# Attention units with transposed sums: which operand of the normalisation is read with a stride

## The chip, the cores and the metric

The kernel runs on one core of a Trainium2 chip. The metric is device time in microseconds (us) of one execution; what is quoted as the time before is the median of three runs. The engines are named as in the profile: PE is TensorE (matmuls), PEld its weight loads, DVE is VectorE, ACT is ScalarE, POOL is GpSimd, SP is SyncE, whose queue issues most DMAs.

## The reference

Everything is bf16, with S = 2048 tokens, D = 512 features, H = 32 heads of Dh = 128, and a key and value cache of 2048 positions for each head.

```python
xn = layernorm(x)                                   # [2048, 512]
q  = (xn @ wq) -> [32 heads, 2048, 128]
p  = softmax(q @ k_cache^T * Dh**-0.5)              # over 2048 keys
s  = (p @ v_cache) -> [2048, 4096] @ wo             # back to [2048, 512]
g  = silu(B(xn))     # B: a token-shifting mixer (w1, w2) and an MLP 512 -> 1792 -> 512 (w3, w4), both residual
out = x + s * g
```

## The kernel before, in words

The first part (until about 130 us) makes `xn`, its transpose `xnT` and most of the gate `g`. The rest is attention, and that is where the change lies.

Attention is cut into 128 units. `units` lists them by group `g` of four heads (8 groups), block `qt` of 512 queries (4 blocks) and head `hh` in the group, the head running fastest. A unit has eight slots. Slot n of the main loop belongs to unit u = n // 8 and has the place p = n % 8 in it. In each slot PE makes two score matmuls for unit u (`s_slot`: keys as weights, `qT` of 128x512 streamed through, into one PSUM tile `ps_s`), ACT takes the exponential of the 128x1024 scores into a tile `pT` (L291), and PE makes two matmuls of an earlier slot with the values as weights (`pv_slot`, into `ps_o`). In the middle part these run ten slots late (`lag = 2 * LAG`). PE's spare places go to the projection of a coming unit's queries (`q_mm`, four matmuls a unit) and to the output projection of finished units (`wo_slot`, `wo_mm`, four matmuls a unit). `pin` fixes the order of each engine: what is written first in the loop is first on its engine, and nothing overtakes.

DVE sums the exponentials: `add_first`, `add_next` and `add_last` (L297, L302, L307, L308) fold a unit's `pT` tiles into `acc[:, 0, :]`, 128 keys by 512 queries. What is still missing is the sum over the 128 partitions, its reciprocal, and that reciprocal spread over all partitions. There are two ways to it. Units outside `TURN` use four tiny matmuls (`sums`). The 96 units of `TURN` (12 to 107, so all of them in whole blocks of four heads) use a DMA transpose: `turn` (L333) transposes `acc` into `tT`, so that query j * 128 + p lies in partition p, place j; `turned_sums` (L338 to L342) sums each row on DVE into `sm`, a 128x4 tile, takes the reciprocal `rc`, and writes it to a DRAM tile `dr`; `bcast` (L346) reads `dr` back as one row of 512 numbers into every partition of `rb`. In that row, query j * 128 + p stands in column p * 4 + j.

`norm` (L358) then multiplies the unit's output `ps_o` (128x512, fp32, in PSUM, queries in their natural order) by `rb` (fp32, in SBUF) and writes bf16 into one quarter of `oT`, which holds the four heads of a block. As the columns of `rb` are ordered p * 4 + j in TURN units, it is read there with a step of four elements; `ps_o` and `oT` are walked in a row. For a TURN unit u the DVE work falls like this: `turn(u)` in slot 3 of unit u + 1, `turned_sums(u)` in slot 0 and `bcast(u)` in slot 1 of unit u + 2, and `norm(u)` in slot 7 of unit u + 2. On DVE, the order around it is: `add_next` of the running unit (slot 6), `norm` (slot 7), `wo_post` of an output tile (L411, slot 7), then at slot 0 of the next unit `turned_sums` of the next unit (L338, L340) and `add_last` (L302, L307, L308), and in slot 3 the copy of the next queries (`q_copy`, L275).

When the four heads of a block are done, `wo_mm` takes, for each 128 tokens `ts` of the block and each head, the columns `ts * P:(ts + 1) * P` of `oT` as matmul weights against `wo`. `ps_o` has two PSUM buffers, so the first `pv_slot` of a unit (slot 2 of unit u + 3 for the buffer of unit u) waits until `norm` of the unit two before has read its buffer. The keys are used as weights with a step as well: `s_slot` views `kT` as `"d (i p j) -> d i j p"` with j = 4, so its 128 weight columns lie four elements apart.

Loads of the next group's keys and values (`load_k`, a DMA transpose, and `load_v`) are issued on SP's queue at set slots around each change of group, between `dr`, `rb` and `tT`.

Of the kernel before, what the change touches and what calls it, by code (L numbers as in the profile page):

```python
# [17 lines left out]
def kernel(  # L18
# [16 lines left out]
    P = nc.NUM_PARTITIONS  # L35
# [9 lines left out]
    QT = Sq // 512  # L45
# [5 lines left out]
    HG = 4  # L51
    NG = H // HG
# [55 lines left out]
    def mm(out, lhsT, rhs, start, stop):  # L108
        pin(nc.tensor.matmul(out=out, lhsT=lhsT, rhs=rhs, start=start, stop=stop))  # L109
# [14 lines left out]
    TURN = range(3 * HG, NU - 5 * HG)  # L124
    PV0, PV1 = 2 * HG, NU - 5 * HG + 3
    NS = NU * SPU
    kTs, vBs, wqs, wos, oTs, st = {}, {}, {}, {}, {}, {}
# [221 lines left out]
    def norm(u):  # L349
        g, qt, hh = units[u]  # L350
        s = st.pop(u)
        if hh == 0:
            oTs[(g, qt)] = pB.tile([P, HG, 512], BF16, tag="oT", bufs=2, name="oT")
        o, rb, to = s["o"][:], s["rb"][:], oTs[(g, qt)][:, hh, :]
        if u in TURN:
            o, to = (x.rearrange("k (j p) -> k j p", j=4) for x in (o, to))
            rb = rb.rearrange("k (p j) -> k j p", j=4)
        pin(nc.vector.tensor_tensor(out=to, in0=o, in1=rb, op=ALU.mult))  # L358

    wo_box = {}  # L360
    sacc = {}

    def load_wo(h):
        wos[h] = pB.tile([P, D], BF16, tag="wo", bufs=2 * HG, name="wo_h")
        pin(nc.sync.dma_start(out=wos[h][:], in_=A_wo[h * Dh:(h + 1) * Dh, :]))

    def wo_mm(g, t, hhs):
        if hhs[0] == 0:
            wo_box[0] = psX.tile([P, D], FP32, tag="xm", name="ps_wo")
        oT = oTs[(g, t // 4)]  # L370
        ts = t % 4
        for hh in hhs:
            mm(wo_box[0][:], oT[:, hh, ts * P:(ts + 1) * P], wos[g * HG + hh][:], hh == 0, hh == HG - 1)

    fin = {}

# [73 lines left out]

    def last_wo(ts, ps, hhs=(0, 1, 2), stop=False):
        for hh in hhs:
            mm(ps, oTs[(NG - 1, QT - 1)][:, hh, ts * P:(ts + 1) * P], wos[(NG - 1) * HG + hh][:],
               hh == 0, stop and hh == HG - 2)

    def last_act(ps, scale):
# [200 lines left out]
    def norm_queue(u):  # L657
        norm(u)
        gg, qq, hh = units[u]
        if hh == HG - 1:  # L660
            wo_todo.extend((gg, 4 * qq + ts) for ts in range(4))
            if gg == NG - 1 and qq not in LATE:
                fin_load(4 * qq)
# [3 lines left out]
    def wo_slot(part, n, each=2):  # L667
        gg, t = wo_todo[0]
        if part < HG // each:
            wo_mm(gg, t, tuple(range(part * each, (part + 1) * each)))  # L670
            return
        wo_todo.popleft()
        wo_post(gg, t, n)
        if gg == NG - 1 and t % 4 < 3 and t + 1 not in fin and t // 4 not in LATE:
            fin_load(t + 1)

    q_plan = defaultdict(list)
    for v in range(1, NU):
        if v not in made:
            for dc in range(DC):  # L680
                k = dc - 1 if v - 2 in TURN else dc // 2
                q_plan[(v - 1) * SPU + k].append((v, (dc,)))

    for n in range(UB * SPU):
        u, p = divmod(n, SPU)
# [45 lines left out]
    for p in range(SPU):  # L731
        s_slot(UB, p)
        pv_run(n + p)
        if p == 0:
            add_last(UA)
        if p < 2:
            wo_slot(p, n + p)
        if p == 3:
            norm(UB - 2)
            sums(UA)  # L740
            wo_slot(2, n + p)
        if p == 4:
            bcast(UA)
            add_first(UB)
        if p == 6:
            add_next(UB, 2)
# [5 lines left out]
    def bank(pl, tag, **kw):  # L752
        return pl.tile([P, D], FP32, tag=tag, name="ps_w", **kw)[:]

    ps = {0: bank(psX, "xm")}
# [6 lines left out]
    late_sums(UB, [acc[:, i, :] for i in range(2)], True, False)  # L762
    late_sums(UB, [pT[:, i, :] for i in range(2, 4)], False, True)
    norm(UA)
    late_rc(UB)
    late_o(UB)
    last_wo(0, ps[0], stop=True)
    late_wo(UB, 0, wl[0])
    wl[1] = bank(psO, "ps_o")
    late_wo(UB, 1, wl[1])  # L770
    last_wo(1, ps[1])
    wl[2] = bank(psX, "xa")
    wl[3] = bank(psO, "ps_o")
# [9 lines left out]
    tb[1] = last_act(wl[1], rc[:, 1:2])  # L783
    tb[2] = last_act(wl[2], rc[:, 2:3])
    last_wo(2, ps[2])
    join(1)
    last_wo(3, ps[3])
# [49 lines left out]
```

## Time and profile before

| | |
|---|---|
| median of three runs | 1260.08 us (1258.32, 1260.08, 1260.21) |
| the profiled execution's own time | 1261.13 us |
| its span in the profile | 1259.4 us |
| PE busy | 1239.5 us, 98% |
| ACT busy | 1100.7 us, 87% |
| DVE busy | 1033.0 us, 82% |
| granted TensorE clock | 0.999 |

The span is what the profile covers from the first to the last instruction; the execution's own time is 1.7 us longer. A line such as `L358 DVE TENSOR_TENSOR oT<-ps_o,rb 128x512` names the source line, the engine, the operation, and the tiles written and read; behind `x` stands the count. A matmul row of some 379 ns is the latency of one matmul; the next one starts long before, so the pitch between starts, not this number, tells how fast PE goes. The stage in which TURN units are normalised goes from about 258 to 1091 us.

### The profile page before, as it was taken

What the parts mean: (1) busy time and instruction counts of PE and PEld (TensorE: products, weight loads), DVE (VectorE), ACT (ScalarE), POOL (GpSimd) and SP (SyncE); (2) the same over time, 40 slices, a digit from 0 to 9 for tenths busy, and PEclk for the clock granted to TensorE, in tenths of its full rate; (3) what the DMA queues carried; (4) which work ended last, traced back from release to release, by engine and by line L of the source; (5) the groups of instructions that cost most, each with busy time, mean ns of one, the idle gap of its engine ahead of it and who ended that gap; (6) DMA issues with size and microseconds to landing.
All of it is one profiled execution on the core that took longest, in us unless ns stands there. A gap on an engine that the chain in (4) does not pass through costs nothing.

```text
span 1259.4 us, 16202 instructions
## 1 busy us (share of the span) xinstructions
PE 1239.5 (98%) x5782; PEld 598.3 (48%) x5899; DVE 1033.0 (82%) x1430; ACT 1100.7 (87%) x1113; POOL 34.4 (3%) x91
## 2 busy tenths in 40 slices
PE   8999999999999999999999999999999999999997
PEld 4444444444444444444444444444444444444443
DVE  7621567788888988888898988988898999988888
ACT  4344889999998999999999999999999999898886
POOL 4320000000000000000000000000000000000000
PEclk9999999999999999999999999999999999999999
DMA  6492012444345423454354524553364434452222
GB/s 155 106 169 72 10 30 46 82 91 93 60 72 97 110 58 76 88 110 84 47 101 94 104 50 76 96 116 69 55 101 102 101 66 82 92 97 54 68 56 59
DMA packets 224945, 103.86 MB, mean 82 GB/s; under 512 B 176928, under 2 KB 208160, under 8 KB 224864
## 3 DMA queue, kind: packets, MB, share of 16 engines
q1 hardware_dynamic: 221648, 100.07, 40.9%
q0 software_dynamic: 672, 1.84, 0.8%
q8 instruction: 46, 0.75, 0.3%
q10 hardware_dynamic: 2544, 0.92, 0.3%
q14 instruction: 35, 0.29, 0.1%
HBM read 67.90 MB, written 2.36 MB: 56 GB/s over the span
## 4 chain that ended last, share of the span: by engine, by line
PE 88%; DMA 5%; DVE 5%; ACT 1%; issue 1%; DVEq 0%; ACTq 0%; SPq 0%
PE ps_s L109 36%; PE ps_o L109 33%; PE ps_q L109 8%; PE ps_wo L109 8%; DMA rb<-dr 3%; PE ps_m L109 2%; DMA dr<-rc 2%; DVE oT L358 1%; DVE acc L302 1%; DVE sacc L411 1%; DVE sm L338 1%; DMA tT<-acc 0%; PE ps_warm L109 0%; ACT pT L291 0%; ACT xnT L199 0%
## 5 line engine op out<-in xcount | busy, mean ns | idle before, releaser
L291 ACT ACTIVATE pT<-ps_s 128x1024 bf16<-128x1024 f32 x1024 | 1034.6, 1023 | 79.1 <-PE ps_s L109 31.4
L109 PE MATMUL ps_s<-qT,kT 128*128 128x512 bf16 x2041 | 607.5, 379 | 0.6
L109 PE MATMUL ps_o<-pT,vb 128*128 128x512 bf16 x1962 | 588.9, 379 | 2.3 <-DVE oT L358 1.8
L302 DVE TENSOR_TENSOR acc<-acc,pT 128x2048 bf16<-128x2048 bf16 x255 | 309.2, 1213 | 73.4 <-ACT pT L291 68.6
L109 PEld LDWEIGHTS <-kT 128*128 128x128 bf16 x2048 | 231.0, 113 | 226.2 <-issue 0.8
L109 PEld LDWEIGHTS <-vb 128*128 128x128 bf16 x2048 | 200.2, 98 | 228.3 <-issue 3.0
L109 PE MATMUL ps_wo<-wo_h,oT 128*128 128x512 bf16 x492 | 177.8, 379 | 2.1
L109 PE MATMUL ps_q<-xnT,wq_h 128*128 128x512 bf16 x481 | 172.7, 379 | 2.1
L297 DVE TENSOR_TENSOR acc<-pT 128x2048 bf16<-128x2048 bf16 x128 | 155.7, 1216 | 6.1 <-ACT pT L291 5.9
L358 DVE TENSOR_TENSOR oT<-ps_o,rb 128x512 bf16<-128x512 f32 x127 | 124.4, 980 | 30.5 <-DMA rb<-dr 29.7
L307 DVE TENSOR_TENSOR acc<-acc 128x1024 bf16<-128x1024 bf16 x127 | 87.9, 692 | 4.3
L275 DVE CAST qT<-ps_q 128x512 bf16<-128x512 f32 x112 | 76.5, 683 | 0.3 <-PE ps_q L109 0.3
L109 PEld LDWEIGHTS <-oT 128*128 128x128 bf16 x508 | 48.5, 98 | 56.6 <-DVE oT L358 1.1
L109 PEld LDWEIGHTS <-wq_h 128*128 128x128 bf16 x484 | 47.2, 98 | 56.2 <-issue 0.2
L411 DVE TENSOR_TENSOR sacc<-ps_wo,sacc 128x512 f32<-128x512 f32 x96 | 65.5, 683 | 3.2 <-PE ps_wo L109 2.7
L338 DVE TENSOR_REDUCE sm<-tT 128x4 f32<-128x512 bf16 x96 | 64.7, 674 | 1.8 <-DMA tT<-acc 1.8
L308 DVE TENSOR_TENSOR acc<-acc 128x512 bf16<-128x512 bf16 x127 | 54.0, 425 | 4.3
L242 ACT ACTIVATE h2T<-ps_s 128x1024 bf16<-128x1024 f32 x28 | 28.6, 1023 | 24.1 <-PE ps_s L109 24.1
L109 PE MATMUL ps_s<-xn2T,w_sb 128*128 128x512 bf16 x219 | 48.6, 379 | 0.3
L109 PEld LDWEIGHTS <-w_sb 128*128 128x128 bf16 x304 | 29.7, 98 | 34.6 <-issue 2.1
L109 PEld LDWEIGHTS <-h2T 128*128 128x128 bf16 x224 | 21.5, 98 | 25.0 <-issue 0.2
L109 PE MATMUL ps_m<-w_sb,h2T 128*128 128x512 bf16 x106 | 31.0, 379 | 0.5
(73 smaller groups left out, 333.5 us busy)
## 6 DMA issues: line engine op xcount, KB each, us to landing
rb<-dr SPq DMA_DIRECT2D x127, 256.0 KB, 4.2
vb<-in_A_v_cache_dram SPq DMA_DIRECT2D x64, 256.0 KB, 3.3
wo_h<-in_A_wo_dram SPq DMA_DIRECT2D x32, 128.0 KB, 3.6
wq_h<-in_A_wq_dram SPq DMA_DIRECT2D x28, 128.0 KB, 3.3
w_sb<-in_B_w_dram SPq DMA_DIRECT2D x9, 256.0 KB, 5.0
kT<-in_A_k_cache_dram SPq DMA_TRANSPOSE x128, 3.3
xl<-in_A_x_dram SPq DMA_DIRECT2D x16, 128.0 KB, 3.7
dr<-rc SPq DMA_DIRECT2D x127, 2.0 KB, 1.4
```

The costliest lines, as they stand in the source:

```text
L109: pin(nc.tensor.matmul(out=out, lhsT=lhsT, rhs=rhs, start=start, stop=stop))
L242: pin(nc.scalar.activation(out=h2[c, f][:], in_=ps[:], func=ACT.Gelu_apprx_tanh))
L275: pin(nc.vector.tensor_copy(out=qT[:], in_=st[u].pop("psq")[:]))
L291: pin(nc.scalar.activation(out=s["pT"][-1][:, jj:jj + 2, :], in_=sps[:], func=ACT.Exp, scale=SCALE))
L297: pin(nc.vector.tensor_tensor(out=s["acc"][:], in0=s["pT"][0][:], in1=s["pT"][1][:], op=ALU.add))
L302: pin(nc.vector.tensor_tensor(out=a[:], in0=a[:], in1=st[u]["pT"][i][:], op=ALU.add))
L307: pin(nc.vector.tensor_tensor(out=a[:, 0:2, :], in0=a[:, 0:2, :], in1=a[:, 2:4, :], op=ALU.add))
L308: pin(nc.vector.tensor_tensor(out=a[:, 0, :], in0=a[:, 0, :], in1=a[:, 1, :], op=ALU.add))
L338: pin(nc.vector.tensor_reduce(out=sm[:], in_=s["tT"][:], axis=mybir.AxisListType.X, op=ALU.add))
L358: pin(nc.vector.tensor_tensor(out=to, in0=o, in1=rb, op=ALU.mult))
L411: pin(nc.vector.tensor_tensor(out=sa, in0=ps[:], in1=sa, op=ALU.add))
```

## The change

In TURN units, `norm` walks all its operands in the order of `rb`: `rb` and the output quarter of `oT` in a row, and `ps_o` with a step of 128 fp32 elements (512 bytes) from one element to the next, four elements to a turn. So the columns of `oT` of a TURN unit stay in the order p * 4 + j. A new function `o_cols` gives `wo_mm` and `last_wo` the 128 columns of a token tile: of a TURN unit every fourth column, of other units the same contiguous slice as before. The number and order of instructions, and what each waits for, stay as they were. `last_wo` handles the last block, which is outside TURN.

```diff
@@ norm
         if u in TURN:
-            o, to = (x.rearrange("k (j p) -> k j p", j=4) for x in (o, to))
-            rb = rb.rearrange("k (p j) -> k j p", j=4)
+            o = o.rearrange("k (j p) -> k p j", j=4)
+            rb, to = (x.rearrange("k (p j) -> k p j", j=4) for x in (rb, to))
         pin(nc.vector.tensor_tensor(out=to, in0=o, in1=rb, op=ALU.mult))
@@
+    def o_cols(g, qt, hh, ts):
+        o = oTs[(g, qt)][:, hh, :]
+        if (g * QT + qt) * HG + hh in TURN:
+            return o.rearrange("k (p j) -> k j p", j=4)[:, ts, :]
+        return o[:, ts * P:(ts + 1) * P]
+
     def wo_mm(g, t, hhs):
...
-        oT = oTs[(g, t // 4)]
         ts = t % 4
         for hh in hhs:
-            mm(wo_box[0][:], oT[:, hh, ts * P:(ts + 1) * P], wos[g * HG + hh][:], hh == 0, hh == HG - 1)
+            mm(wo_box[0][:], o_cols(g, t // 4, hh, ts), wos[g * HG + hh][:], hh == 0, hh == HG - 1)
@@ last_wo
-            mm(ps, oTs[(NG - 1, QT - 1)][:, hh, ts * P:(ts + 1) * P], wos[(NG - 1) * HG + hh][:],
+            mm(ps, o_cols(NG - 1, QT - 1, hh, ts), wos[(NG - 1) * HG + hh][:],
```

## The prediction

> **What bounds the kernel now.** I read the page's busy times first, then the stage of the TURN units (a window from the first to the last `turned_sums`), PE's timeline in it, the waits, and last the chain of waits.
>
> ```profile
> span 1259.4 us, 16202 instructions
> ...
> PE 1239.5 (98%) x5782; PEld 598.3 (48%) x5899; DVE 1033.0 (82%) x1430; ACT 1100.7 (87%) x1113; POOL 34.4 (3%) x91
> ```
>
> ```profile
> 258.40:1083.50 825.10, 819.31 (x3738) 396.35 (x3813) 732.34 (x966) 779.72 (x763) 0.00 (x0) 1.00 0.45 86
> ```
>
> The second row's columns after the length are PE, PEld, DVE, ACT and POOL busy with counts, granted clock, DMA share, GB/s. PE is busy in 819.31 of 825.10 us at a granted clock of 1.00, DVE in 732.34. A busy PE need not be at its peak, so the pitch of its matmuls has to be read:
>
> ```profile
> 599.53 0.59 PE L109 MATMUL ps_s<-qT,kT 128*128 128x512 bf16 x2
> 599.96 0.59 PE L109 MATMUL ps_o<-pT,vb 128*128 128x512 bf16 x2
> 600.40 0.38 PE L109 MATMUL ps_q<-xnT,wq_h 128*128 128x512 bf16 x1
> 600.61 0.59 PE L109 MATMUL ps_s<-qT,kT 128*128 128x512 bf16 x2
> 601.04 0.59 PE L109 MATMUL ps_o<-pT,vb 128*128 128x512 bf16 x2
> 601.48 0.38 PE L109 MATMUL ps_wo<-wo_h,oT 128*128 128x512 bf16 x1
> 601.69 0.59 PE L109 MATMUL ps_s<-qT,kT 128*128 128x512 bf16 x2
> 602.12 0.38 PE L109 MATMUL ps_o<-pT,vb 128*128 128x512 bf16 x1
> ```
>
> From 599.53 to 602.12 start 2+2+1+2+2+1+2 = 12 matmuls: 216 ns each, the same for every kind of weight. A unit has 16 score, 16 value, 4 query and 4 output matmuls, so 40 x 0.216 = 8.63 us. DVE's turn in the same place:
>
> ```profile
> 602.30 1.22 DVE L297 TENSOR_TENSOR acc<-pT 128x2048 bf16<-128x2048 bf16 x1
> 604.46 1.22 DVE L302 TENSOR_TENSOR acc<-acc,pT 128x2048 bf16<-128x2048 bf16 x1 [0.93 <-ACT pT L291]
> 605.60 1.07 DVE L358 TENSOR_TENSOR oT<-ps_o,rb 128x512 bf16<-128x512 f32 x1
> 606.60 0.68 DVE L411 TENSOR_TENSOR sacc<-ps_wo,sacc 128x512 f32<-128x512 f32 x1
> 607.20 0.67 DVE L338 TENSOR_REDUCE sm<-tT 128x4 f32<-128x512 bf16 x1
> ...
> 610.93 1.22 DVE L297 TENSOR_TENSOR acc<-pT 128x2048 bf16<-128x2048 bf16 x1
> ```
>
> One unit takes 610.93 - 602.30 = 8.63 us here too, and DVE idles 0.93 us of it, waiting for ACT. So PE's stream sets the pace, without a gap, and DVE has 0.93 us a unit to spare. Time can be won only where PE itself waits. The waits from 258 to 1092 us name those places (us in total, times, longest):
>
> ```profile
> DVE oT L358 <- DMA rb<-dr: 25.6, 38, 2.6
> ...
> PE ps_o L109 <- DVE oT L358: 1.8, 2, 1.6
> ...
> PE ps_sum L109 <- DVE qT L275: 0.7, 1, 0.7
> ```
>
> The first row matters only through the second: `norm` waits 38 times for its broadcast, but PE waits for `norm` twice. The two larger stalls by PE's starts:
>
> ```profile
> 399.21 0.59 PE L109 MATMUL ps_s<-qT,kT 128*128 128x512 bf16 x2
> 401.40 0.59 PE L109 MATMUL ps_o<-pT,vb 128*128 128x512 bf16 x2 [1.60 <-DVE oT L358]
> ...
> 1086.67 0.59 PE L109 MATMUL ps_o<-pT,vb 128*128 128x512 bf16 x2
> 1087.92 0.27 PE L109 MATMUL ps_sum<-ones_t,acc 128*128 128x1 bf16 x4 [0.66 <-DVE qT L275]
> ```
>
> Two matmuls after 399.21 the next was due at 399.64 and came at 401.40: 1.76 us lost. Likewise it was due at 1087.10 and came at 1087.92: 0.82 lost. The other wait for `norm` is 1.8 - 1.6 = 0.2. All that DVE costs PE in this stage is 0.2 + 1.76 + 0.82 = 2.8 us.
>
> **The change, part by part.** (1) *The multiply of `norm`.* Its duration in units 0 to 11 (nothing strided) and in the 96 TURN units (`rb` read with a 16-byte step), from the answers for line L358 in the two stages (ns, min/median/max):
>
> ```profile
> L358 DVE TENSOR_TENSOR oT<-ps_o,rb x12: 678/682/684, 151.4 to 252.8; 128x512 bf16<-128x512 f32 x12
> ...
> L358 DVE TENSOR_TENSOR oT<-ps_o,rb x96: 1054/1073/1094, 267.8 to 1090.3; 128x512 bf16<-128x512 f32 x96
> ```
>
> The strided SBUF read costs 1073 - 682 = 391 ns, 0.76 ns for each of 512 elements. The change takes it away and puts a read of PSUM with a 512-byte step in its place. No row of this trace reads PSUM with a step. From below: 682 ns, the step free; less than that is excluded, since 682 is the price with all three operands in a row. From above, the nearest row is `rb`'s own step: 1073 again; were a longer hop twice as dear, 682 + 2 x 391 = 1464. I take 682: the read of PSUM is another memory's, and in the 12 unstrided rows it is not what the multiply waits for, since the add of L411 above, also 128x512 with one operand in PSUM, takes the same 0.68 us. That is the weakest step, and both ends go into the range. At 682, DVE loses 96 x 0.391 = 37.5 us of busy time, nearly all of it behind PE.
>
> [...]
>
> (2) *What is late next.* A shorter `norm` brings everything behind it on DVE forward: `wo_post` (L411), `turned_sums` (L338, L340), and so the issue of `dr` and `rb` on SP. The chain of waits shows that these close a ring ahead of the 1.76 us stall:
>
> ```profile
> 335.78 0.99 DVE oT L358
> 336.77 0.60 DVE sacc L411
> 337.37 0.60 DVE sm L338
> 338.20 1.39 DMA dr<-rc
> 339.61 5.82 DMA rb<-dr
> 345.45 1.08 DVE oT L358
> ...
> 395.00 5.27 DMA rb<-dr
> 400.29 1.07 DVE oT L358
> ```
>
> Each `norm` starts when `rb` lands, and its end releases the sum that the next `rb` needs. From 345.45 to 400.29 there are six turns of 9.14 us against PE's 8.63: the ring falls behind while key and value loads share the queues, until PE waits. With 0.39 us less a turn it takes 8.75; six turns end 2.3 us earlier and the last `norm` 0.39 earlier still, more than the 1.76 lost. This supposes that `rb` lands earlier when issued earlier. If the landing is held by the loads around it, only the last `norm` counts: 0.39. At 1087 us the wait is for the query copy (L275), which stands behind `norm` on a DVE without idle time: 0.39 of 0.82 certain, more if that `rb` too comes earlier. The wait of 0.2 goes.
>
> (3) *The weights of the output projection.* 24 blocks x 4 token tiles x 4 heads = 384 loads read every fourth column. The keys are read with the same step:
>
> ```profile
> L109 PEld LDWEIGHTS <-kT x2048: 110/113/120, 127.1 to 1245.1; 128*128 128x128 bf16 x187
> ...
> L109 PEld LDWEIGHTS <-oT x380: 97/98/98, 262.3 to 1079.3; 128*128 128x128 bf16 x190
> ```
>
> Such a load takes 113 in place of 98 ns, 15 more, and lies beside a matmul of 216: in PE's timeline above, matmuls on `kT` start at the same pitch as the rest. I take nothing; if that cover were gone, 384 x 0.015 = 5.8 us. No load can get shorter. (4) The bf16 write stays in a row, and no DMA, wait or order changes: nothing.
>
> Sum: lowest gain 0.2 + 0.39 + 0.39 = 1.0 us, highest 2.8; I take 0.2 + 1.76 + 0.39 = 2.35. Against the profiled execution's own 1261.13 us (1.7 of it outside the span) that is 1258.8. The shown runs have their median at 1260.08 and the fastest at 1258.32, as far under 1261.13 as these stalls are long (2.8), so I read the runs' differences as more or less of the same stalls. A median without most of them stands at about **1258.7**, 1.4 under the median now.
>
> **The rivals.** *The PSUM read costs what the SBUF read did*: `norm` stays near 1073 and nothing moves, 1260.1. For it speaks that the step is longer than `rb`'s; against it, that it is another memory. *The read is dearer than before, and the ring falls further behind*: at 1464 each turn of the ring takes 0.39 more, so the stall at 399 grows by 7 x 0.39 = 2.7 and the other two by 0.39 each: 3.5 more, 1260.08 + 3.5 = 1263.6, slower; it decides from any duration over 1073. [...] *DVE becomes the bound*: over 1.07 + 0.93 = 2.0 us of `norm`, DVE's turn passes 8.63 and all 96 units pay; at 682 + 4 x 391 = 2246 ns that is 96 x 0.24 = 23 us, 1283. Nothing in the trace shows a price that high. *The strided weights stall PE*: 1260.08 + 5.8 = 1265.9; the rows of `kT` speak against it, and for it only that an output load sits singly between other kinds.
>
> **How the numbers follow.** The forecast, a free PSUM step, gets 0.55; the same price 0.16; the dearer read 0.12; the DVE bound 0.06; the weights 0.11. The forecast alone ranges from 1261.13 - 2.8 = 1258.3 to 1261.13 - 1.0 = 1260.1. The range goes down to 1257.2, as a run may vary by about another 1 us below that, as the three shown do among themselves, and up to 1263.6, which leaves out the DVE bound and the weights (0.17). About 0.2%, 2.5 us, is what a measurement of this kernel can tell from no change. In the forecast a gain over that comes only if all stalls go and the runs before are like the profiled one (2.8 of 1261.13 is 0.22%): 0.20 of its 0.55, the rest is same. The second rival is same; of the dearer read 0.10 is slower, of the weights 0.09, the DVE bound wholly. Faster 0.20; slower 0.10 + 0.06 + 0.09 = 0.25; same 0.55.
>
> **What would show it.** Right: the TURN rows of L358 at about 682, DVE busy near 995 us, weights from `oT` at about 113 ns with PE's pitch still 216, the wait of PE for L358 gone, the idle time of L302 behind ACT longer. Wrong: L358 at 1073 or above, PE waiting for L358 more than twice, a pitch over 216 around `ps_wo`; or L358 at 682 and the stall near 399 us still there, which would say that `rb`'s landing, not its issue, closes the ring.

## The result and the profile after

The kernel after takes 1258.01 us (median of 21 runs, 1257.45 to 1259.76) where the kernel before, in the same comparison, takes 1260.06 (21 runs, 1258.32 to 1262.11): ratio 0.9985, 95% interval 0.9979 to 0.9991. That is 2.0 us less, clear of noise and within 0.2%. The profiled executions took 1261.13 before and 1258.32 after.

The page's head, after (span, then busy time, share and count of each engine):

```profile
span 1256.5 us, 16202 instructions
...
PE 1238.1 (99%) x5782; PEld 604.2 (48%) x5899; DVE 997.1 (79%) x1430; ACT 1100.6 (88%) x1113; POOL 34.4 (3%) x91
```

DVE is busy 36 us less (1033.0 to 997.1), and the span is 2.9 us shorter. The multiply, from the answer for its line from 258 to 1092 us, its last instance being one outside TURN (ns, min/median/max), and the loads from `oT` in the same window:

```profile
L358 DVE TENSOR_TENSOR oT<-ps_o,rb x97: 676/684/693, 268.4 to 1091.6; 128x512 bf16<-128x512 f32 x97
...
L109 PEld LDWEIGHTS <-oT x384: 97/113/116, 262.4 to 1086.0; 128*128 128x128 bf16 x192
```

So the PSUM read with a step of 512 bytes costs nothing: 684 ns against 682 with all operands in a row. The weight loads went from 98 to 113 ns. The waits of that window, after (us in total, times, longest):

```profile
DVE acc L302 <- ACT pT L291: 78.0, 89, 0.9
DVE acc L297 <- ACT pT L291: 23.6, 68, 0.8
DVE oT L358 <- DMA rb<-dr: 10.6, 13, 1.5
```

No row is left in which PE waits for DVE. The freed time stands in the first two rows, where DVE waits for ACT. `norm` waits for `rb` 13 times in place of 38. The chain of waits from 330 to 405 us, before and after, tells the rest; its head gives the share of each line:

```profile
by line: DMA rb<-dr 41.6%; DMA dr<-rc 20.6%; DVE oT L358 9.6%; DVE sacc L411 5.9%; DVE sm L338 5.6%; PE ps_s L109 4.0%; PE ps_o L109 3.7%; issue 2.4%; DVE rc L340 1.8%; DVE acc L302 1.6%; ACT pT L291 1.4%; PE ps_wo L109 1.2%; PE ps_q L109 0
```

```profile
by line: PE ps_s L109 40.3%; PE ps_o L109 38.0%; PE ps_wo L109 11.2%; PE ps_q L109 10.2%; issue 0.5%
```

Before, the chain there went through the ring of `norm`, sums and broadcast; after, it is PE's stream alone. DVE's timeline, after, at the two ends of the six units that took 9.14 us each before:

```profile
345.14 0.69 DVE L358 TENSOR_TENSOR oT<-ps_o,rb 128x512 bf16<-128x512 f32 x1 [0.60 <-DMA rb<-dr]
...
396.26 0.68 DVE L358 TENSOR_TENSOR oT<-ps_o,rb 128x512 bf16<-128x512 f32 x1
```

The first of these `norm`s waited 0.60 us for its broadcast. Six units on this is made up: 51.12 us against PE's 6 x 8.63 = 51.78. The pace of the ring itself can't be read from them, as `norm` hardly waits for `rb` any more. The answers for `rb` from 330 to 405 us, before and then after (DVE's waits in us and times; time from issue to landing):

```profile
  DMA rb<-dr: 8.4, 7
...
DMA to landing us min/median/max: 3.5/4.2/5.8
```

```profile
  DMA rb<-dr: 0.6, 1
...
DMA to landing us min/median/max: 3.3/3.5/5.8
```

The broadcasts themselves landed faster in the profile after. Not all of that is the work of the shorter `norm`: in e1_weights below, whose `norm` still takes 1073 ns, the median there is 3.6. The stalls at 399 and at 1087 us are gone (PE's timeline, after):

```profile
399.26 0.59 PE L109 MATMUL ps_o<-pT,vb 128*128 128x512 bf16 x2
...
1084.53 0.59 PE L109 MATMUL ps_o<-pT,vb 128*128 128x512 bf16 x2
1084.96 0.27 PE L109 MATMUL ps_sum<-ones_t,acc 128*128 128x1 bf16 x4
```

The first sums of a unit outside TURN start 0.43 us after the two matmuls ahead of them, at PE's pitch. The rows also tell where the 2.9 us were won. The matmul that came at 401.40 before comes at 399.26, 2.14 earlier, and the sums that came at 1087.92 come at 1084.96, 2.96 earlier: 2.1 us up to the first place, 0.8 from there to the second, and nothing behind it.

### The profile page after: what moved, and what is told of

Read it like the earlier page. It is cut to its first block, busy times and chain, and to the rows that moved or that the text cites. A ratio compares the mean times of both kernels' runs of the same rounds, so it can differ in the third digit from the quotient of the medians.

```text
span 1256.5 us, 16202 instructions
## 1 busy us (share of the span) xinstructions
PE 1238.1 (99%) x5782; PEld 604.2 (48%) x5899; DVE 997.1 (79%) x1430; ACT 1100.6 (88%) x1113; POOL 34.4 (3%) x91
## 4 chain that ended last, share of the span: by engine, by line
PE 95%; DVE 2%; DMA 1%; ACT 1%; issue 1%; POOL 0%; SPq 0%; DVEq 0%; ACTq 0%
PE ps_s L109 39%; PE ps_o L109 36%; PE ps_q L109 9%; PE ps_wo L109 9%; PE ps_m L109 2%; DVE acc L302 0%; PE ps_sum L109 0%; ACT qT L277 0%; ACT xnT L199 0%; DMA rb<-dr 0%; DMA wq_e<-in_A_wq_dram 0%; DMA dr<-rc 0%; PE ps_w L109 0%; DMA xin<-in_A_x_dram 0%; DVE xall L425 0%
## 5 line engine op out<-in xcount | busy, mean ns | idle before, releaser
L358 DVE TENSOR_TENSOR oT<-ps_o,rb 128x512 bf16<-128x512 f32 x127 | 86.9, 685 | 14.9 <-DMA rb<-dr 13.0
L109 PEld LDWEIGHTS <-oT 128*128 128x128 bf16 x508 | 54.6, 110 | 56.6 <-DVE oT L358 1.2
```

## The experiments

The theory: the gain is `norm`'s 0.39 us at its place in the ring, which let PE's few waits go. The rivals: the other order of columns or the weights moved PE; DVE's total load decides; or only the last `norm` counts, as `rb` lands when the loads let it. Where an added line shifts the numbering, `norm` is L359, PE's helper L110, and the extra add L665.

**The weights alone.**

```diff
 # before, with norm as it was
-            mm(wo_box[0][:], oT[:, hh, ts * P:(ts + 1) * P], ...)
+            mm(wo_box[0][:], o_cols(g, t // 4, hh, ts), ...)
```

> The kernel before with one half of the change: the output projection loads its weights with a step of four columns, norm stays as it was (so tokens of a block come out in another order than the reference's). Theory (the gain is norm's shorter time on the ring of norm, sums and broadcast; the weight load is hidden beside a matmul): the time of before, 1260.1, loads from oT at 113 ns, pitch of PE 216 ns, norm at 1073 ns, PE still waiting for norm. Rival (the strided loads move PE's stream): up to 5.8 us slower, 1265.9, or if the gain came from the loads, 1258.

Measured: 1259.45 us against 1258.78 of before, ratio 1.0001 (0.9992 to 1.0010). PE's timeline:

```profile
600.00 0.59 PE L109 MATMUL ps_s<-qT,kT 128*128 128x512 bf16 x2
600.43 0.59 PE L109 MATMUL ps_o<-pT,vb 128*128 128x512 bf16 x2
600.86 0.38 PE L109 MATMUL ps_wo<-wo_h,oT 128*128 128x512 bf16 x1
...
602.59 0.59 PE L109 MATMUL ps_o<-pT,vb 128*128 128x512 bf16 x2
```

The elided rows bring it to twelve starts in 2.59 us, 216 ns: the strided weights leave PE's pitch as it was, and the time shows no change clear of noise, which here is about 1 us. In this execution PE had no recorded wait for `norm`, so the 1.76 us stall at 399 us of the first profile is not in every execution with a `norm` of 1073 ns. The stall at the end of the stage is there:

```profile
1086.06 0.59 PE L109 MATMUL ps_o<-pT,vb 128*128 128x512 bf16 x2
1087.38 0.27 PE L109 MATMUL ps_sum<-ones_t,acc 128*128 128x1 bf16 x4 [0.72 <-DVE qT L275]
```

Due at 1086.49, the sums came 0.89 us late. This execution (1260.91 us) also lost time elsewhere: its first load of keys as weights starts at 128.8 us, where the profiles before and after have 127.1 and 127.2.

**The saved time put back, in the ring and out of it.** A spare DVE add whose result nobody reads, once in each of the 96 units, at two places.

```diff
 # after; e2_ring: behind norm            # e3_off: behind add_first, slot 4
+    nc.vector.tensor_tensor(out=spare[:], in0=xnT[:, 0, 0:608], in1=xnT[:, 1, 0:608], op=ALU.add)
```

> The kernel after with one extra DVE add (128x608 bf16, some 0.47 us long, 0.39 us of pitch) directly behind norm in each TURN unit: the 0.39 us that the change saved is put back at the same place of the ring. Theory (ring): the time of before, 1260.1, and PE waits for norm again by 1.5 to 3 us in total near the changes of group. Rival (the gain comes from the order of columns, the strided access or the weights): stays at 1258.0.

> The kernel after with the same extra add, put behind add_first in slot 4, where DVE then idles before the next sum: DVE gets the same busy time as in e2_ring, but outside the ring. Theory (ring): stays at 1258.0 and PE does not wait for norm. Rival (DVE's total load decides): 1260.1 as in e2_ring.

Measured, on one chip with before at 1258.78: in the ring 1259.66 us (1258.15 to 1260.86; ratio 1.0005, 0.9996 to 1.0014), out of it 1258.09 (1257.59 to 1258.44; ratio 0.9990, 0.9982 to 0.9999). By the pages' heads DVE is busy 1031.6 us in the ring and 1033.3 out of it, as much as before (1033.0); the place differs, and with it the time. PE's waits for DVE from 258 to 1092 us, in the ring; out of it there is none:

```profile
PE ps_sum L110 <- DVE qT L276: 1.3, 1, 1.3
...
PEld L110 <- DVE acc L309: 0.6, 1, 0.6
...
PE ps_o L110 <- DVE oT L359: 0.4, 1, 0.4
```

So at this load the place decides, not the sum of DVE's work, and the column order or the strided access is not the gain: with both in place, the add behind `norm` takes it back. But the expected wait for `norm` of 1.5 to 3 us near the changes of group did not come back. All of PE's waits lie after 1020 us, most of them at the query copy. From about 965 us on, each unit has one more DVE step (L389 or L394 here). DVE's timeline there, in the ring:

```profile
1063.40 0.69 DVE L359 TENSOR_TENSOR oT<-ps_o,rb 128x512 bf16<-128x512 f32 x1 [2.65 <-DMA rb<-dr]
...
1071.76 0.68 DVE L359 TENSOR_TENSOR oT<-ps_o,rb 128x512 bf16<-128x512 f32 x1
```

`norm` waits 2.65 us for one late broadcast, and DVE then works without a pause, 8.36 us a unit. That is only 0.27 under PE's 8.63, so the delay is not made up before the query copy, for which PE waits. In e3_off DVE's turn there is shorter, although its busy time is the same (1052.52 to 1061.16, less 0.39 idle: 8.25 us). So the pair shows the place to matter; how much of it is the ring and how much DVE's own turn, it does not part.

**The ring made longer than before.** The same add behind `norm` in the kernel before.

> The kernel before with the same extra add (0.39 us of pitch) directly behind norm in each TURN unit, so that norm and the add stand for a multiply of 1464 ns. Theory (ring): each turn of the ring takes 0.39 us more, the stalls grow as the prediction's rival of a dearer read has it, 1 to 4 us over before, with PE waiting for norm by 3 us or more. Rival (the steady part has 0.93 us of DVE to spare, so nothing happens): the time of before.

Measured: 1263.23 us against 1259.04, ratio 1.0032 (1.0020 to 1.0043), 4.2 us more. DVE's wait for ACT and PE's waits for DVE in the window:

```profile
DVE acc L303 <- ACT pT L292: 24.4, 49, 0.9
...
PE ps_sum L110 <- DVE qT L276: 1.7, 1, 1.7
PE ps_o L110 <- DVE oT L359: 1.6, 3, 0.8
PEld L110 <- DVE acc L309: 1.0, 1, 1.0
```

Two windows, up to 976 us and after it (columns as in the prediction), and `norm` in the second:

```profile
258.00:976.00 718.00, 718.00 (x3327) 346.37 (x3326) 663.07 (x913) 680.36 (x667) 0.00 (x0) 1.00 0.43 85
976.00:1092.00 116.00, 112.77 (x521) 53.80 (x520) 111.69 (x159) 105.36 (x104) 0.00 (x0) 1.00 0.41 83
```

```profile
1011.31 1.07 DVE L359 TENSOR_TENSOR oT<-ps_o,rb 128x512 bf16<-128x512 f32 x1
...
1020.05 1.07 DVE L359 TENSOR_TENSOR oT<-ps_o,rb 128x512 bf16<-128x512 f32 x1
```

A read price of 1464 ns would have made this change a loss, but not in the way that the theory had it. Up to 976 us PE loses nothing, at 399 us either, though each turn of the ring holds 0.39 us more; DVE's 49 idle times of the first row all lie there. The loss lies after 976 us. There DVE's turn is 1020.05 - 1011.31 = 8.74 us without a pause, over PE's 8.63: DVE itself has become the bound, and three late broadcasts (1.7 us of waits) come on top. The expected wait of 3 us or more for `norm` alone was not met: 1.6, the rest at the end of the stage.

**The ring cut otherwise.** Sums ahead of `norm`, with the strided `rb`.

```diff
 # before
-        if p == 0 and u - 2 in TURN:
-            turned_sums(u - 2)
...
+        if p == 7 and u - 1 in TURN:
+            turned_sums(u - 1)
         if p == (7 if u - 2 in TURN else 2 + late) and 2 <= u:
             norm_queue(u - 2)
```

> The kernel before (norm at 1073 ns, strided rb) with the ring cut in another way: turned_sums of unit u - 1 is issued in slot 7 ahead of norm of unit u - 2, not in slot 0 behind it, so dr is issued some 1.6 us earlier and no longer waits for norm. Theory (rb lands earlier when it is issued earlier): PE's waits for norm go, 1258.0 to 1258.7, with norm still at 1073. Rival (rb's landing is held by the key and value loads, only norm's own length counts): the stall near 399 us stays, 1260.1. A possible new wait: DVE for the transposed sums tT, which has one slot less to land.

Measured: 1267.76 us, ratio 1.0071 (1.0058 to 1.0084): slower. The waits from 258 to 1092 us:

```profile
DVE acc L302 <- ACT pT L291: 62.6, 78, 0.9
DVE sm L338 <- DMA tT<-acc: 25.2, 20, 2.9
...
PE ps_o L109 <- DVE oT L358: 8.4, 9, 1.7
```

No row is left in which `norm` waits for `rb` (25.6 us in 38 waits before): the broadcast lands in time when its numbers are sent off earlier, which speaks against the rival, though `norm`, now behind the sums on DVE, also starts later. But the sums now wait for `tT` (25.2 us), and `norm` is late for PE nine times. A wait was exchanged for a worse one; this cut does not show what a free ring is worth.

**More load, in and out of the ring.**

> The kernel after with three extra adds (1.17 us of pitch in all) behind add_first in slot 4 of each unit that normalises a TURN unit, outside the ring; DVE's busy time then passes that of before by some 70 us. Theory (ring; DVE has about 1.3 us a unit to spare after the change): 1258 to 1259. Rival (DVE's load decides): slower than before, by 2 us or more.

> The kernel after with the three extra adds directly behind norm, in the ring (a multiply of about 1.85 us): the same DVE work as e6_off3 in another place. Theory (ring): a turn of the ring near the changes of group takes about 9.9 us against PE's 8.63, with hardly any time to catch up between, so PE waits for norm by 5 to 20 us in all, 1263 to 1278 us. Rival (only DVE's load decides): the same time as e6_off3.

> The kernel after with five extra adds (1.95 us) at the same place outside the ring. Both theories: DVE's turn passes PE's 8.63 us by about 0.6 us (1.95 less the 1.3 to spare), 96 units pay it, 1258 + 60 = 1318 us. It measures where DVE becomes the bound, which the prediction put at a norm of 2.0 us.

Measured against 1259.04 of before: three adds out of the ring 1266.48 us (1.0059, 1.0047 to 1.0072), three in it 1312.43 (1.0422, 1.0408 to 1.0436), five out of it 1358.10 (1.0782, 1.0765 to 1.0798). All three were slower than the theory had said, and three adds out of the ring came out as the rival had it. The windows of three adds out of the ring (columns as in the prediction):

```profile
500.00:700.00 200.00, 200.00 (x928) 97.70 (x927) 195.49 (x302) 189.55 (x186) 0.00 (x0) 1.00 0.45 90
976.00:1091.00 115.00, 110.56 (x505) 52.99 (x504) 112.88 (x176) 102.73 (x101) 0.00 (x0) 1.00 0.38 80
```

From 500 to 700 us PE has no gap although DVE is busy 195.5 of 200. From 976 us on, PE loses time: there each unit has one more DVE step.

```profile
1012.68 1.22 DVE L303 TENSOR_TENSOR acc<-acc,pT 128x2048 bf16<-128x2048 bf16 x1
...
1018.11 0.68 DVE L389 SCALAR_TENSOR_TENSOR sacc<-sacc,xall 128x512 f32<-128x512 f32 x1
...
1020.45 1.49 DVE L665 TENSOR_TENSOR spare<-xnT 128x608 bf16<-128x608 bf16 x3
1021.85 1.22 DVE L303 TENSOR_TENSOR acc<-acc,pT 128x2048 bf16<-128x2048 bf16 x1
```

DVE's turn is 1021.85 - 1012.68 = 9.17 us without a pause, 0.54 over PE's 8.63. The three adds hold DVE for 1021.85 - 1020.45 = 1.40 us, not the 1.17 that three times the single pitch made. So DVE has 8.63 - (9.17 - 1.40) = 0.86 us to spare for work in slot 4 here. With five adds all 96 units are bound by DVE:

```profile
599.94 1.22 DVE L298 TENSOR_TENSOR acc<-pT 128x2048 bf16<-128x2048 bf16 x1
601.07 2.50 DVE L665 TENSOR_TENSOR spare<-xnT 128x608 bf16<-128x608 bf16 x5
603.49 1.22 DVE L303 TENSOR_TENSOR acc<-acc,pT 128x2048 bf16<-128x2048 bf16 x1
...
610.66 2.50 DVE L665 TENSOR_TENSOR spare<-xnT 128x608 bf16<-128x608 bf16 x5
```

A turn is 9.59 us, of which the adds hold 2.42; without them 7.17, so after the change DVE has 8.63 - 7.17 = 1.46 us to spare for work in slot 4 of the steady part. Three adds in the ring cost 46 us more than the same adds out of it. PE's waits from 258 to 1092 us, in the ring:

```profile
DVE oT L359 <- DMA rb<-dr: 22.6, 44, 2.4
PE ps_wo L110 <- DVE sacc L417: 17.8, 60, 0.3
PE ps_o L110 <- DVE oT L359: 6.4, 12, 2.0
```

The place behind `norm` is also ahead of `wo_post` (L417 here), which frees the one PSUM buffer of `ps_wo`: 60 of PE's waits are for that. And DVE's own turn is longer with the adds in this place:

```profile
607.99 0.69 DVE L359 TENSOR_TENSOR oT<-ps_o,rb 128x512 bf16<-128x512 f32 x1
...
614.30 1.22 DVE L298 TENSOR_TENSOR acc<-pT 128x2048 bf16<-128x2048 bf16 x1
615.62 1.23 DVE L303 TENSOR_TENSOR acc<-acc,pT 128x2048 bf16<-128x2048 bf16 x1
616.82 0.69 DVE L359 TENSOR_TENSOR oT<-ps_o,rb 128x512 bf16<-128x512 f32 x1
```

It is 616.82 - 607.99 = 8.83 us without a recorded wait, over PE's 8.63. The two adds into `acc` start 1.32 us apart here (614.30 to 615.62); with spare adds between them the first held DVE for 1.13 (599.94 to 601.07 above). So the same adds cost DVE 0.19 us a unit more behind `norm` than in slot 4. In this run DVE is the bound in the steady part too, and the 46 us are no price of the ring.

**A step further.** With DVE time free, more units can take their sums by the DMA transpose and spare PE four tiny matmuls each. In the profile after, the matmul behind such a four starts 0.13 us after the first of them (1160.82 to 1160.95).

```diff
 # after
-    TURN = range(3 * HG, NU - 5 * HG)     # 12 to 107
+    TURN = range(8, 112)                  # also range(8, 120) and range(8, 108)
```

> The kernel after, unchanged, on the chip of the next two runs. Theory (its stage has no stall left that could vary): 1258.0, with a narrower spread than before, and no wait of PE for norm.

> The kernel after with TURN from 8 to 111 in place of 12 to 107: eight more units take the sums by the transposing DMA, which takes four tiny matmuls of about 0.16 us in all from PE for each, and puts 0.84 us of sums on DVE. Theory (the shorter norm has left DVE some 1.3 us and the ring about as much): 8 x 0.16 = 1.3 us less than after, 1256.7. Rival (in these units the ring or DVE is late, since the value matmuls there run closer behind): PE waits for norm or for the sums, 1258 to 1262.

> The same with TURN from 8 to 119, sixteen units more than after, the first half of the last group among them. Theory: 16 x 0.16 = 2.6 us less than after, 1255.4. Rival: as the lag of the value matmuls shrinks there from ten slots to five, norm in slot 7 and its broadcast come too late for the last blocks: over 1258.

> The kernel after with TURN from 8 to 107: only the four early units of the eight in e11_turn_8_112, whose stalls all lay behind unit 107. Theory: four times 0.16 us of tiny matmuls less than after's 1258.0, some 0.2 lost in one wait for norm near 267 us: 1257.4 to 1257.8. Rival: the value matmuls run less far behind in units 8 to 11, so PE waits there for more than it saves, 1258.0 or over.

Measured: after again 1257.99 us (1257.57 to 1258.52) with before at 1258.81 (0.9992, 0.9984 to 1.0001). TURN to 111: 1260.87 (1.0016, 1.0008 to 1.0025); to 119: 1295.92 (1.0294, 1.0280 to 1.0308). TURN from 8 to 107: 1258.05 with before at 1258.82 (0.9993, 0.9984 to 1.0003), no different from after. The kernel after did as expected, with runs 0.95 us apart at most where those of before were 2.8; the gains expected of the other three did not come, and their rivals had it. PE in the kernel with TURN to 111:

```profile
1096.44 0.59 PE L109 MATMUL ps_s<-qT,kT 128*128 128x512 bf16 x2
1097.92 0.59 PE L109 MATMUL ps_o<-pT,vb 128*128 128x512 bf16 x2 [0.88 <-DVE oT L358]
```

In the late units `norm` in slot 7 comes too late for value matmuls that run fewer slots behind: from 1092 to 1130 us PE waits for it four times, 3.3 us in all, and in the kernel with TURN to 119 (from 100 us on) 13 times, 27.3 us. No version tried beats the kernel after.

## Why the prediction was right

It forecast 1258.7 us, 1.4 under before; measured were 1258.01 and 2.0. The price of the read and the direction are right. That the sum comes so close is luck in part, as the size of its largest term belonged to one execution.

- **What bounds the kernel.** Right. Two matmuls start 0.43 us apart after as before, and 36 us less of DVE work brought 2 us.
- **The multiply.** The weakest step held: 684 ns against 682 assumed. The reason given for it could not carry it, though: the add of L411 reads its PSUM operand in a row like the 12 unstrided rows, so none of them tells what a step costs there. What the step of 16 bytes costs on `rb` in SBUF (1073 ns against 682) does not carry over to the step of 512 bytes on `ps_o` in PSUM (684 ns); only the run with that step shows it.
- **The ring.** Right that the time behind `norm` is what counts: the pair e2_ring and e3_off shows the place to matter. The traces bear out, too, that an earlier issue lands earlier: from 258 to 1092 us the median from issue to landing is 4.2 us before and 4.0 after, so the broadcasts that are issued earlier do not wait longer to land. What the prediction read wrongly is the pace of 9.14 us before the 1.76 us stall. Its chain holds two broadcasts of 5.04 and 5.27 us; in e1_weights, with the same `norm`, and in e5_ring_before, with a longer one, PE lost nothing at 399 us. The 1.76 us are thus of that execution, and how many runs of before have such a stall is not known.
- **The sum.** The term for 1087 us was too small: 0.39 taken, all of 0.82 gained. This stall is the steadier one: e1_weights has it with 0.89 us, and the profiles of after, e3_off and e10_after_again have no wait of PE there. With a `norm` of 1073 ns DVE has little time left in these units: in e1_weights 8.37 us from `norm` to `norm` without a pause (1064.02 to 1072.39), in the kernel after 8.41 of which 0.55 are idle (1069.88 to 1078.29). So a late broadcast is made up sooner. In the two profiled executions all 2.8 us of PE's waits went, 1261.13 to 1258.32; the median, 1258.01, lies 0.3 below the floor of 1258.3 that was read from them.
- **The size against before** was 2.0 us in the first comparison and 0.8 in that of e10_after_again, where the interval up to 1.0001 does not quite part it from no change. What moves is before, at 1260.06 first and 1258.8 to 1259.0 in the later comparisons, while after stood at 1258.0 both times. The stall at 1087 us alone is worth 0.8 us, which would fit the later ones; that is not shown, and why before differs was not settled. The prediction read the differences between runs as more or less of the same stalls; e1_weights, with 1.6 us lost ahead of attention, shows another part.
- **The weights.** Right: 113 ns, no loss.
- **The rivals.** The same price, which the prediction counts as its second rival, is out: the multiply takes 684 ns, not 1073. The dearer read was priced at 3.5 us, most of it at 399 us; e5_ring_before measured 4.2, all of it after 976 us. The number agrees, the way to it does not. The point at which DVE becomes the bound was put at a `norm` of 2.0 us for all units. After the change there are 1.46 us to spare in slot 4, less the 0.19 that work behind `norm` adds: 0.68 + 1.27 = 1.95 in the steady part, as predicted, but 0.68 + 0.86 - 0.19 = 1.35 in the units after 976 us, whose extra step the prediction overlooked. The 1.07 + 0.39 = 1.46 us of e5_ring_before are over that, and its turn of 8.74 us shows it.

## What to carry to other kernels

When PE's matmuls stand at their pitch, look up the few places where PE waits and follow each back: here 36 us less of DVE work, off the busiest engine, brought 2.0, won where `norm` stood on the way to such a wait. The same 0.39 us counted behind `norm` (1259.66 us) and not in slot 4 (1258.09), so test a gain by putting the time back at both places. Look where in the run the side engine has least time left: here one more DVE step a unit after 976 us decided where the added time was lost (turns of 8.74 us in e5_ring_before, 9.17 in e6_off3, against PE's 8.63). Take a stall of one execution as its own until a second execution shows it. Where a two-operand VectorE instruction must permute one operand, measure the step on the PSUM side before putting it on an SBUF operand of four-byte elements (684 ns against 1073 here).

## What the runs showed of the hardware

A VectorE multiply of 128x512 reads fp32 from PSUM with a step of 512 bytes in 684 ns (after), hardly more than in a row (682), while a step of 16 bytes on its fp32 SBUF operand makes it 1073 (before). Identical VectorE adds to the same tile, one behind another, took about 0.5 us each (2.42 for five in e7_off5) where a single one between other work took 0.38 (603.63 to 604.01 us in e2_ring). The add L303, which reads what L298 writes, started 1.32 us behind it (e9_ring3); an add into another tile started 1.13 us behind L298 (e7_off5). Weights of 128x128 bf16 read with a step of four columns load in 113 ns (after) in place of 98 (before), and PE's pitch stays at 216 ns (e1_weights).
